# Moving one batch's loads to the SyncE queue and placing every block of loads behind the last transposes of the batch before

## The chip, the cores and the metric

The kernel runs on one core of one Trainium2 chip. The metric is the device time of one launch in microseconds; the kernel before took 297.23 us (median of three runs: 297.23, 308.93 and 295.3). Lower is better.

## The reference

Two stages follow each other. The first is a linear attention with cosine position weights, on 8 batches of 8 heads, 576 positions and head size 64. The second is a feed-forward layer with a squared ReLU.

```python
r = np.maximum(x, 0.0)                       # x is q or k
phi = np.concatenate([r * cos, r * sin], -1)  # 64 -> 128 features
kv = np.einsum('bhsf,bhsd->bhfd', k_p, v)
z = np.sum(k_p, axis=2)
num = np.einsum('bhsf,bhfd->bhsd', q_p, kv)
den = np.einsum('bhsf,bhf->bhs', q_p, z)[..., None] + 1e-06
attn = num / den                              # [8, 8, 576, 64]
x = attn.transpose(0, 2, 1, 3).reshape(4608, 512)
out = np.maximum(x @ w_in, 0.0) ** 2 @ w_out  # 512 -> 2048 -> 512
```

q, k and v hold 9.4 MB each, the two weights 4.2 MB each, and the output 9.4 MB, all in float32.

## The kernel before, in words

**Tiling.** One batch at a time goes through everything. Its 576 positions are cut into four blocks of 128 (the main part) and a tail of 64. The main part of q, k or v is one transfer of 1 MB; the tail is two transfers of 64 KB. There is one buffer each for k, v, q and their tails (`POOLS`, "k": 1 and so on), so the loads of a batch can start only once the features of the preceding batch have been read out of these buffers.

**Attention of a batch (`declare_att`).** VectorE and ScalarE make the cosine and sine features of k and q and cast v to bf16 (`declare_feature`, `declare_v`). TensorE forms the product of k features and v (`declare_kz`), and ScalarE copies it out (`kvz`). The q features must be turned round so that features lie on partitions: for batch 2 and later a DMA transpose on the SyncE queue does this (`declare_qT`, L531: two of 512 KB and one small one, `qpT` and `qpTt`). TensorE then forms numerators and denominators (`declare_num`), VectorE divides and writes `x`, and `x` is turned round by DMA transposes again (`declare_xT`, L620: two of 256 KB and a small one, `xT` and `xTt`). Batches 0 and 1 use TensorE transposes instead.

**Feed-forward of a batch.** Stage one (times `T1[b]`) multiplies `xT` by the first weight, stage two (times `T2[b]`) multiplies the squared ReLU `gT` by the second. Batches 0 to 2 use plain products in stage one (`declare_plain`), later ones a scheme with seven products instead of eight (`declare_seven1`, fed by the sums `xs` of `declare_x_sums`); stage two has rows (`declare_rows`) for the first and pairs with seven products (`declare_pair`) for the rest. In time the attention of batch b+2 lies beside stage two of batch b and stage one of batch b+1.

**Order.** Nothing here is ordered by hand. Each operation is declared with its engine, an estimated duration, the buffers it reads and writes, and for some a position in time (`pos`). `Planner.plan` then goes through them as a list scheduler and emits them in the order of its own clock; after that every engine runs its list in order, and waits on semaphores where data is not there. If an estimate is wrong, an engine stands at the head of its list while later work that is ready waits behind. For DMA the planner has one line of transfers (`pipe`) for all queues: each transfer begins when the one before is done.

**Queues.** Loads come from two places. Loads of batches 0 to 3 go out from GpSimd's queue (q0 in the profile, software_dynamic), except the k of batch 0; the loads of batches 4 to 7 go out from SyncE's queue (q1, hardware_dynamic), which also carries all DMA transposes. The output stores go out from GpSimd's queue, except at the very end. The loads carry a `pos`: batch 3 is declared at `T2[0] + 10`, the k and v of batch b+2 at `T2[b-1] + 10` and its q at `T1[b] + 8.7`; before that time the planner doesn't place them, and from then on it places them as soon as their buffer is free.

Of the kernel before, what the change touches and what calls it, by code (L numbers as in the profile page):

```python
# [34 lines left out]
class Planner:  # L35
# [19 lines left out]
        self.turns.setdefault(pool, []).append(b)  # L55
        return b

    def add(self, engs, fn, r=(), w=(), pos=None, lat=None, size=None):
        if isinstance(engs, tuple):
            engs = {engs[0]: engs[1]}  # L60
        if size:
            lat = 1.5 + size
        op = Op(engs, fn, pos, lat, size)
        for k in r:
            if k in self.writer:
                op.deps.add(self.writer[k])
            self.readers.setdefault(k, []).append(op)
        for k in w:
            if k in self.writer:
                op.deps.add(self.writer[k])  # L70
            op.deps.update(x for x in self.readers.get(k, ()) if x is not op)
            self.writer[k], self.readers[k] = op, []
        for k in list(r) + list(w):
            b = k[0] if isinstance(k, tuple) else k
            if isinstance(b, Buf) and b not in op.bufs:
                op.bufs.append(b)
                b.users += 1
        self.ops.append(op)
        return op

# [26 lines left out]
    def plan(self, t0):  # L107
        ops = self.ops
        for n, op in enumerate(ops):
            op.n = n  # L110
            for d in op.deps:
                d.succ.append(op)
        pe = sorted((o for o in ops if "PE" in o.engs), key=lambda o: (o.pos, o.n))
        t = t0["PE"]
        for o in pe:
            o.late = o.slot = t
            t += o.engs["PE"]
        for o in reversed(ops):
            d = max(o.engs.values()) + (o.lat or 0.16)
            for s in o.succ:  # L120
                o.late = min(o.late, s.late - d)
            if "PE" not in o.engs:
                ends = [
                    s.slot + s.engs["PE"]
                    for s in o.deps
                    if "PE" in s.engs and any(b in s.bufs for b in o.bufs if b.pool in "FB")
                ]
                if ends:
                    o.late = min(o.late, max(ends) + 1.0)
        clock = dict(t0)  # L130
        waiting = {o: len(o.deps) for o in ops}
        pipe = 0.0
        ready = {e: [] for e in clock}
        order = []

        def arm(o):
            for e in o.engs:
                ready[e].append(o)

        for o in ops:  # L140
            if not o.deps:
                arm(o)
        left = len(ops)
        head = 0
        while left:
            best = None
            while head < len(pe) and pe[head].start is not None:
                head += 1
            for e in clock:
                cand = []  # L150
                for o in ready[e]:
                    if e == "PE" and o.slot > pe[head].slot + self.window:
                        continue
                    s = max(clock[e], o.pos if e not in ("PE",) and o.pos else 0.0)
                    for d in o.deps:
                        s = max(s, d.end if d.eng == e and e in ("PE", "ACT", "DVE") else d.done)
                    s = self.room(o, s)[0]
                    if s is not None:
                        cand.append((s, o))
                if not cand:  # L160
                    continue
                s0 = min(c[0] for c in cand)
                s, o = min(
                    (c for c in cand if c[0] <= s0 + 1e-9),
                    key=lambda c: (c[1].slot if e == "PE" else c[1].late, c[1].n),
                )
                if best is None or s < best[0]:
                    best = (s, e, o)
            if best is None:
                stuck = [o for o in pe if o.start is None][:6]  # L170
                raise RuntimeError(f"stuck: {[(o.fn.__name__, o.pos, o.n) for o in stuck]}")
            s, e, o = best
            for x in o.engs:
                ready[x].remove(o)
            o.eng, o.start, o.end = e, s, s + o.engs[e]
            o.done = o.end + (o.lat if o.lat is not None else 0.17 if e == "PE" else 0.09) + self.HOP
            if o.size:
                pipe = o.done = max(o.end + 1.5, pipe) + o.size
            clock[e] = o.end
            for b, i in self.room(o, s)[1]:  # L180
                b.i = i
                self.free[b.pool] = [f for f in self.free[b.pool] if f[1] != i]
            for b in o.bufs:
                b.users -= 1
                b.last = max(getattr(b, "last", 0.0), o.done)
                if b.users == 0:
                    self.free[b.pool].append((b.last, b.i))
            for x in o.succ:
                waiting[x] -= 1
                if not waiting[x]:  # L190
                    arm(x)
            order.append(o)
            left -= 1
        return order
# [3 lines left out]
def kernel(  # L198
# [17 lines left out]
    J = S // P  # L216
# [186 lines left out]
    add = plan.add  # L403
# [6 lines left out]
    T1, T2, t = {}, {}, 16.8  # L410
# [8 lines left out]
            d[key] = plan.buf(pool)  # L419
        return d[key]  # L420

    def declare_load(b, nm, eng, pos=None):
        src = {"k": k, "v": v, "q": q}[nm]
        queue = nc.sync if eng == "SP" else nc.gpsimd
        for part, fn, cost, size in ((nm, load_main, 0.7, 2.9), (nm + "t", load_tail, 1.4, 0.7)):
            buf = loaded[part, b] = plan.buf(part)

            def load(_, fn=fn, buf=buf):
                fn(src, nm, buf.i, b, queue)

            add((eng, cost), load, w=[buf], pos=pos, size=size)

    def source(nm, b, j):
        return loaded[nm if j < J else nm + "t", b]
# [22 lines left out]
    def xT_of(b, half):  # L457
        return cached(xTb, (b, half), "xT")
# [64 lines left out]
    def declare_qT(b, i):  # L523
        n = 2 if i < J // 2 else 1
        src = qp_of(b, 2 * i)
        dst = qpTb[b, i] = plan.buf("qpT" if n == 2 else "qpTt")

        def qT(_):
            s = at(src)
            s = s.rearrange("p r h f -> p (r h f)" if n == 2 else "p h f -> p (h f)")  # L530
            nc.sync.dma_start_transpose(out=at(dst), in_=s)  # L531

        keys = [(src, (2 * i + r) % 2, c) for r in range(n) for c in "cs"]
        add(("SP", 1.7 if n == 2 else 1.2), qT, r=keys, w=[dst], size=1.8 if n == 2 else 0.5)

    def declare_qT_pe(b, j, pos, engs):
        nh = H if j < J else HH
# [65 lines left out]
    def declare_xT(b, i):  # L603
        src = x_of(b, 2 * i)
        if i < J // 2:
            dst, keys = xT_of(b, i), [(src, 0), (src, 1)]
            wkeys = [(dst, 0), (dst, 1)]
        else:
            dst, keys = xTt_of(b), [(src, 0)]
            wkeys = [(dst, b % 4)]  # L610

        def xT(_):
            if i < J // 2:
                o = at(dst).rearrange("p k (r c) -> p (k r) c", r=2)
                s = at(src).rearrange("p k r c -> p (k r c)")
            else:
                o = at(dst)[:, b % 4].rearrange("p k g c -> p (k g) c")
                o = at(dst)[:, b % 4].rearrange("p k g c -> p k (g c)")
                s = at(src).rearrange("p k c -> p (k c)")
            nc.sync.dma_start_transpose(out=o, in_=s)  # L620

        add(("SP", 1.6 if i < J // 2 else 1.2), xT, r=keys, w=wkeys, size=1.0 if i < J // 2 else 0.5)

    def declare_xT_pe(b, j, pos, engs):
        nk = KB if j < J else 2
# [61 lines left out]
            r=[rt], w=[gkey(hb, half)],  # L687
        )

    gttb = {}  # L690

    def declare_tails(b, hb, pos):

# [444 lines left out]
            declare_plain(1, s % 4 * 4 + 2 * i, s // 4, T1[1] + s * 2 * PROD2 + i * PROD2, s == 0)  # L1138
    declare_att(2, T2[1], [T2[1] + x for x in (1.7, 3.4, 5.1, 7.0, 9.0)], DVE1, DVE1, BOTH)
    for nm in "qkv":  # L1140
        declare_load(3, nm, "POOL", T2[0] + 10)
    declare_rows(1, (0, 1), T2[1], 2)
    declare_w2_sums()
    declare_pair(1, 1, T2[1] + 16 * PROD1)
# [5 lines left out]
    for b in range(2, B):  # L1150
        if b > 2:
            if b in SEVEN:
                declare_x_sums(b)
                for r in range(4):
                    declare_seven1(b, r, T1[b] + r * 7 * PROD1)
            for m, first, n in TAILS[b]:
                for i in range(first, first + n):
                    declare_tails(m, 2 * i, T2[b] - 1.5 + 0.01 * i)
        if b + 2 < B:
            for nm in "kv":  # L1160
                declare_load(b + 2, nm, "SP", T2[b - 1] + 10)
            declare_load(b + 2, "q", "SP", T1[b] + 8.7)
            declare_att(b + 2, T2[b] + 5.5, [T1[b + 1] + 0.3 + 1.75 * j for j in range(NS)])
        for i, pair in enumerate(PAIRS[b]):
            declare_pair(b, pair, T2[b] + i * 7 * PROD2)
# [35 lines left out]
```

## Time and profile before

| what | value |
|---|---|
| three runs | 297.23, 308.93, 295.3 us |
| span of the profiled execution | 311.6 us (that run took 313.36 us) |
| TensorE matmul busy | 276.9 us, 89% of the span |
| VectorE, ScalarE, GpSimd busy | 219.3, 191.3, 46.1 us |
| q1 (SyncE's queue) | 63104 packets, 26.22 MB, 44.5% of the 16 DMA engines' time |
| q0 (GpSimd's queue) | 10544 packets, 26.22 MB, 29.8% |

The busy shares are means over the whole span. TensorE is the busiest engine, and the work is laid out around it, so what counts is where TensorE stands still and why. In the rows with forty slices each digit stands for 7.8 us. The row PEclk gives the clock that TensorE was granted; it falls where TensorE has stood still, and matmuls then take longer. In timelines, the bracket at the end of a line says how long the engine was idle before it and whose work ended that.

### The profile page before, as it was taken

To read this page: it belongs to the slowest core of one execution; us is meant where nothing else is said; L and a number is where in the kernel's file an instruction comes from. 1 tells how busy PE (TensorE), PEld (TensorE's weight loads), DVE (VectorE), ACT (ScalarE), POOL (GpSimd) and SP (SyncE) were. 2 spreads that over 40 slices of the span, in tenths; PEclk is the share of its full clock that TensorE was granted. 3 is DMA by queue.
4 is the path that set the end of the run, shared out by engine and by line. 5 is a ranking of instruction groups with operands and counts; after the bars stand their busy time and mean duration, and the time that the engine had idled before them with its cause. 6 is when DMAs were issued, how large, how long until landed. Compare 5 with 4: busy or idle time off the path is not lost.

```text
span 311.6 us, 7075 instructions
## 1 busy us (share of the span) xinstructions
PE 276.9 (89%) x2827; PEld 226.8 (73%) x2827; DVE 219.3 (70%) x513; ACT 191.3 (61%) x378; POOL 46.1 (15%) x76
## 2 busy tenths in 40 slices
PE   8699999991199948987999989989999999999994
PEld 3379756881048936876878878878888887888883
DVE  2669999950275508937998599869984789449851
ACT  3576917960386647618997995699532673386421
POOL 8625272620000000000000000010002000000012
PEclk9999999998579979999999999999999999999999
DMA  7999997899949998699979997955803520110014
GB/s 242 294 206 326 290 307 246 274 140 174 99 76 215 259 166 199 127 210 373 199 163 250 233 179 155 358 135 140 141 14 105 120 43 2 67 69 2 1 69 135
DMA packets 73825, 53.02 MB, mean 170 GB/s; under 512 B 50496, under 2 KB 68416, under 8 KB 73792
## 3 DMA queue, kind: packets, MB, share of 16 engines
q1 hardware_dynamic: 63104, 26.22, 44.5%
q0 software_dynamic: 10544, 26.22, 29.8%
q8 instruction: 22, 0.36, 0.5%
q10 hardware_dynamic: 144, 0.13, 0.1%
q14 instruction: 11, 0.09, 0.1%
HBM read 36.70 MB, written 9.44 MB: 148 GB/s over the span
## 4 chain that ended last, share of the span: by engine, by line
PE 47%; DMA 25%; DVE 17%; ACT 4%; issue 3%; SPq 2%; POOL 2%; POOLq 0%; DVEq 0%; ACTq 0%
PE banks L395 45%; DMA v<-in_v_dram 10%; DMA vt<-in_v_dram 7%; DMA q<-in_q_dram 5%; DVE gT L384 4%; DVE gs L392 2%; DVE rs L387 2%; DVE qp L373 2%; DMA xTt<-xt 1%; ACT rt L381 1%; SPq L531 1%; DVE x L592 1%; DVE w1s L392 1%; ACT rs L381 1%; PE banks L544 1%
## 5 line engine op out<-in xcount | busy, mean ns | idle before, releaser
L395 PEld LDWEIGHTS <-w1sb 128*128 128x128 bf16 x784 | 73.5, 99 | 15.2 <-DMA xT<-x 4.3
L395 PE MATMUL banks<-xT,w1sb 128*128 128x256 bf16 (+1 forms) x576 | 70.0, 270 | 4.7 <-DMA xT<-x 4.0
L395 PE MATMUL banks<-w2sb,gT 128*128 128x256 bf16 (+1 forms) x304 | 52.8, 315 | 13.7 <-ACT rt L381 13.2
L395 PEld LDWEIGHTS <-gT 128*128 128x128 bf16 x408 | 38.8, 99 | 27.9 <-issue 17.4
L395 PEld LDWEIGHTS <-gs 128*128 128x128 bf16 x480 | 46.4, 98 | 10.2 <-issue 4.1
L381 ACT ACTIVATE rt<-banks 128x512 bf16<-128x512 f32 x64 | 37.2, 597 | 19.9 <-PE banks L395 13.7
L356 POOL DMA_DIRECT2D out_dram<-ysb x15 | 8.3, 551 | 218.3 <-DVE ysb L392 112.8
L395 PEld LDWEIGHTS <-w1s 128*128 128x128 bf16 x320 | 30.7, 98 | 6.9 <-issue 3.2
L384 DVE TENSOR_TENSOR gT<-rt 128x512 bf16<-128x512 bf16 x48 | 19.5, 419 | 22.4 <-ACT rt L381 22.2
L395 PE MATMUL banks<-w2sb,gs 128*128 128x256 bf16 x240 | 31.0, 273 | 3.6 <-DVE ysb L392 1.9
L395 PE MATMUL banks<-w2s,gs 128*128 128x256 bf16 x240 | 30.2, 273 | 0.2
L384 DVE TENSOR_TENSOR gT<-rs 128x1024 bf16<-128x1024 bf16 (+1 forms) x50 | 28.3, 579 | 2.4 <-ACT rs L381 1.8
L387 DVE CUSTOM_DVE_ANT_0 rs<-banks,sums 128x512 bf16<-128x512 f32 x40 | 27.1, 684 | 3.3 <-ACT sums L793 2.5
L392 DVE TENSOR_TENSOR ysb<-banks,sums 128x256 f32<-128x256 f32 x30 | 12.6, 420 | 20.6 <-ACT sums L907 10.3
L378 ACT CAST vx<-v 128x512 bf16<-128x512 f32 x22 | 13.6, 623 | 18.6 <-DMA v<-in_v_dram 18.6
L381 ACT ACTIVATE rs<-banks 128x512 bf16<-128x512 f32 x40 | 23.2, 608 | 2.8 <-PE banks L395 2.8
L371 ACT ACTIVATE kp<-k,sin_col 128x512 bf16<-128x512 f32 x32 | 22.0, 721 | 3.4 <-DMA k<-in_k_dram 3.4
L395 PE MATMUL banks<-xT,w1s 128*128 128x256 bf16 x160 | 22.3, 272 | 1.9 <-DVE rs L387 1.7
L371 ACT ACTIVATE qp<-q,sin_col 128x512 bf16<-128x512 f32 x32 | 22.9, 729 | 1.9 <-DMA q<-in_q_dram 1.7
L395 PE MATMUL banks<-xs,w1s 128*128 128x256 bf16 x160 | 23.4, 273 | 0.0
L592 DVE TENSOR_TENSOR x<-banks,den 128x512 bf16<-128x512 f32 x30 | 20.7, 691 | 1.0
L392 DVE TENSOR_TENSOR gs<-gT 128x1024 bf16<-128x1024 bf16 x26 | 17.9, 688 | 2.8 <-PE banks L395 2.3
(106 smaller groups left out, 382.1 us busy)
## 6 DMA issues: line engine op xcount, KB each, us to landing
out_dram<-ysb POOLq DMA_DIRECT2D x15, 512.0 KB, 5.5
k<-in_k_dram SPq DMA_DIRECT2D x5, 1024.0 KB, 6.0
v<-in_v_dram POOLq DMA_DIRECT2D x4, 1024.0 KB, 12.7
v<-in_v_dram SPq DMA_DIRECT2D x4, 1024.0 KB, 9.4
q<-in_q_dram SPq DMA_DIRECT2D x4, 1024.0 KB, 8.0
q<-in_q_dram POOLq DMA_DIRECT2D x3, 1024.0 KB, 9.4
k<-in_k_dram POOLq DMA_DIRECT2D x3, 1024.0 KB, 7.7
w1sb<-in_moe_w_in_dram POOLq DMA_DIRECT2D x4, 512.0 KB, 9.2
```

The source lines that it names most:

```text
L356: eng.dma_start(out=dst, in_=y.rearrange("p i c -> p (i c)") if n > 1 else y[:, c0:c1])
L371: nc.scalar.activation(out=dst, in_=src, func=ACTF.Relu, scale=col)
L373: nc.vector.tensor_scalar(out=dst, in0=src, scalar1=0.0, scalar2=col, op0=ALU.max, op1=ALU.mult)
L378: (nc.scalar.copy if eng == "ACT" else nc.vector.tensor_copy)(out=out, in_=in_)
L381: nc.scalar.activation(out=out, in_=in_, func=ACTF.Relu)
L384: nc.vector.tensor_tensor(out=out, in0=in_, in1=in_, op=ALU.mult)
L387: nc.vector._custom_dve(TENSOR_ADD_SAT, out=out, in0=in0, in1=in1, s0=float("inf"), s1=0.0)
L392: nc.vector.tensor_tensor(out=out, in0=in0, in1=in1, op=op)
L395: nc.tensor.matmul(out=out, lhsT=lhsT, rhs=rhs, start=start, stop=stop, skip_group_check=True)
L531: nc.sync.dma_start_transpose(out=at(dst), in_=s)
L544: nc.tensor.transpose(t[:, h, :], qp_at(b, j)[:, h, :], ident[:, :])
L592: nc.vector.tensor_tensor(out=x_at(b, j).rearrange("p (b k) (l d) -> p b k l d", b=n, l=2), in0=n4[:, :, :, 0:D].rearrange("p b (k l) d -> ...
```

## The change

The loads of batch 3 move from GpSimd's queue to SyncE's. And no load from batch 3 on has a position in time any more: the k and v loads of batch b+2 are declared to come after the last q transpose of batch b+1 (`turned["q", b + 1, J // 2]`, the small `qpTt`), and its q load after the last x transpose of batch b+1 (`turned["x", b + 1, J // 2]`, the small `xTt`). For batch 3, all of k, v and q come after the last q transpose of batch 2, which is the first batch with DMA transposes. The aim is that loads and transposes lie in one queue, one block behind the other, instead of running beside each other.

`after` is an order for the planner alone: it reads `d.end`, the time at which the preceding transpose has been issued, not the time at which it has landed, and no buffer is shared by it. So it adds no wait on the chip beyond the place in SyncE's list.

```diff
-    def add(self, engs, fn, r=(), w=(), pos=None, lat=None, size=None):
+    def add(self, engs, fn, r=(), w=(), pos=None, lat=None, size=None, after=()):
...
+        op.after = set(after) - op.deps
+        op.deps |= op.after
         self.ops.append(op)
...
                     for d in o.deps:
-                        s = max(s, d.end if d.eng == e and e in ("PE", "ACT", "DVE") else d.done)
+                        ordered = d in o.after or d.eng == e and e in ("PE", "ACT", "DVE")
+                        s = max(s, d.end if ordered else d.done)
...
-            add((eng, cost), load, w=[buf], pos=pos, size=size)
+            add((eng, cost), load, w=[buf], pos=pos, size=size, after=after)
...
-        add(("SP", 1.7 if n == 2 else 1.2), qT, r=keys, w=[dst], size=1.8 if n == 2 else 0.5)
+        turned["q", b, i] = add(("SP", 1.7 if n == 2 else 1.2), qT, r=keys, w=[dst], size=1.8 if n == 2 else 0.5)
...
-        add(("SP", 1.6 if i < J // 2 else 1.2), xT, r=keys, w=wkeys, size=1.0 if i < J // 2 else 0.5)
+        turned["x", b, i] = add(("SP", 1.6 if i < J // 2 else 1.2), xT, r=keys, w=wkeys, size=1.0 if i < J // 2 else 0.5)
...
     for nm in "qkv":
-        declare_load(3, nm, "POOL", T2[0] + 10)
+        declare_load(3, nm, "SP", after=[turned["q", 2, J // 2]])
...
             for nm in "kv":
-                declare_load(b + 2, nm, "SP", T2[b - 1] + 10)
-            declare_load(b + 2, "q", "SP", T1[b] + 8.7)
+                declare_load(b + 2, nm, "SP", after=[turned["q", b + 1, J // 2]])
+            declare_load(b + 2, "q", "SP", after=[turned["x", b + 1, J // 2]])
```

What this does to SyncE's list of instructions can be read from the built kernels. Before, from batch 2 on: the two `qpT` and the `qpTt` of batch 2, `vt` of batch 4, `xT` of 2, `qpT` of 3, k and v of 4, `xT` of 2, `qpT` and `qpTt` of 3, `kt` of 4, q and `qt` of 4, `xTt` of 2, `xT` of 3, and so on, with loads and transposes mixed. After: the three q transposes of 2, then k, v, q, `kt`, `vt`, `qt` of 3 in one block, `xT` of 2, `qpT` of 3, `xT` of 2, `qpT` and `qpTt` of 3, then k, v, `kt`, `vt` of 4, then `xTt` of 2 and the x transposes of 3, then q and `qt` of 4, then the q transposes of 4, and so on. (The one exception to whole blocks: an `xT` of batch 4 lies between q and `qt` of batch 5.) GpSimd's list loses the nine transfers of batch 3 and keeps the earlier loads, the weights and the stores. The lists of the other engines keep their work and change a little in order.

More of the change, by code (lines that the diff above doesn't have):

```diff
@@ L420, in cached, with declare_load @@
         return d[key]
-    def declare_load(b, nm, eng, pos=None):
+    def declare_load(b, nm, eng, pos=None, after=()):
         src = {"k": k, "v": v, "q": q}[nm]
@@ L688, in declare_plain @@
         )
-    gttb = {}
+    gttb, turned = {}, {}
     def declare_tails(b, hb, pos):
```

## The prediction

> **What bounds the kernel now.** I read the forty slices of the page first, then the chain that ended last, then the timelines of TensorE, ScalarE, GpSimd and SyncE at the places where the slices show a hole.
>
> ```profile
> PE   8699999991199948987999989989999999999994
> PEclk9999999998579979999999999999999999999999
> DMA  7999997899949998699979997955803520110014
> PE 47%; DMA 25%; DVE 17%; ACT 4%; issue 3%; SPq 2%; POOL 2%; POOLq 0%; DVEq 0%; ACTq 0%
> ```
>
> TensorE is full nearly everywhere. The one deep hole is in slices 10 and 11 (70 to 86 us), a shallow one in slice 14 (109 to 117 us), and after each its clock is down. DMA is full up to slice 25, and a quarter of the chain is DMA. So the kernel is bound by TensorE, with DMA nearly as full in its first two thirds; what can be won is TensorE's waits. The timelines of TensorE and ScalarE show who ends them:
>
> ```profile
> 84.54 2.72 PE L395 MATMUL banks<-w2sb,gT 128*128 128x512 bf16 x6 [13.22 <-ACT rt L381]
> 90.59 1.89 PE L395 MATMUL banks<-w2sb,gT 128*128 128x512 bf16 x8
> 113.45 1.72 PE L395 MATMUL banks<-xT,w1sb 128*128 128x256 bf16 x8 [3.98 <-DMA xT<-x]
> ...
> 82.58 0.62 ACT L378 CAST vx<-v 128x512 bf16<-128x512 f32 x1 [14.01 <-DMA v<-in_v_dram]
> ```
>
> TensorE waits 13.22 us for a ReLU on ScalarE that had its input long before; ScalarE stood at the cast of batch 3's v, one place ahead in its list, 14.01 us for the load. The load and what shares the DMA engines with it (GpSimd's timeline, then SyncE's, then an undisturbed stretch of SyncE's):
>
> ```profile
> 58.54 1.15 POOL L323 DMA_DIRECT2D v<-in_v_dram  x1 [2.66 <-ACT rt L381]
> 62.14 0.91 POOL L323 DMA_DIRECT2D q<-in_q_dram  x1
> ...
> 57.15 26.52 SPq L531 DMA_TRANSPOSE qpT<-qp  x2
> 83.76 2.59 SPq L531 DMA_TRANSPOSE qpTt<-qpt  x1
> 97.56 1.12 SPq L323 DMA_DIRECT2D v<-in_v_dram  x1
> 98.77 6.08 SPq L620 DMA_TRANSPOSE xT<-x  x1
> 104.96 8.02 SPq L531 DMA_TRANSPOSE qpT<-qp  x1
> ...
> 216.41 6.53 SPq L531 DMA_TRANSPOSE qpT<-qp  x2
> ```
>
> v is issued at 58.5 and read at 82.6: 24 us for 1 MB. In the same stretch SyncE hands out two q transposes and needs 26.52 us for it; later the same pair takes 6.53 us with its waits. Loads on q0 and transposes on q1 run beside each other there, and both crawl. The second wait (3.98 us) is `xT` of batch 2, issued at 98.77 behind k and v of batch 4 on one queue. What DMA moves in each case, by windows (the last three columns are TensorE's clock, the DMA share and GB/s):
>
> ```profile
> 62.00:70.00 8.00, 8.00 (x81) 7.09 (x79) 4.77 (x12) 5.13 (x9) 2.29 (x4) 1.00 1.28 149
> 78.00:84.50 6.50, 0.00 (x0) 0.00 (x0) 0.77 (x2) 1.92 (x5) 0.00 (x0) 0.50 1.24 103
> 99.20:106.00 6.80, 6.80 (x80) 6.16 (x78) 2.76 (x7) 3.56 (x7) 0.56 (x1) 1.00 0.99 302
> 217.60:220.20 2.60, 2.60 (x27) 2.33 (x25) 2.57 (x7) 2.60 (x6) 0.00 (x0) 1.00 1.08 201
> ```
>
> Mixed: 149 and 103 GB/s with engines over full. Loads alone (k and v of batch 4): 302. One q transpose alone: 201, so 0.52 MB in 2.6 us.
>
> **What the Trainium skill says.** "DMA: Bandwidth & Descriptors", section "Queues, rings and completion order": each DMA engine goes round the queue rows that have work, a packet at a time. The trace agrees in kind: a transpose consists of packets under 512 B (50496 of 73825 packets on the page are), and beside another queue it waits a turn for each; that the total rate halves as well goes beyond fair turns. The same page, "Issuing engines are not separate DMA queues": transfers from all issuing engines share 16 DMA engines, so a second queue adds no rate. Agrees: 149 GB/s with two, 302 with one. "TensorE: Matmul & The Clock Gate", "Part 1: The HAM clock gate": after an idle window of about 3.4 us the array's clock is halved until it has been busy as long. Agrees: 8 matmuls of 128x512 take 1.89 us at 90.59, and 6 take 2.72 at 84.54.
>
> **The change part by part.**
>
> *Removed: the first wait, and the half clock behind it.* The wait is 13.22 us. At half clock, 6 wide matmuls took 2.72 instead of 6/8 x 1.89 = 1.42, and the next 8 took 3.00 instead of 1.89; with eight small ones (0.64 for 0.41) that is 2.6. Together 15.9 us.
> Now the new order of this stretch, by hand. The q features of batch 2 are ready at 61.7 as before. Two q transposes at 2.6 us and the small one at about 0.65 (a quarter), the first behind the output stores until about 62, end near 68. k, v, q at 1.05 MB / 302 GB/s = 3.5 us each reach 71.5, 75 and 78.5, the six tails at about 0.2 us 80. The cast of v is now placed behind ScalarE's ReLUs and the copy of `kvz`, and behind three k features, which it would reach at about 72 + 3 x 0.6 = 74. Remaining wait: 0 to 2 us, and no ReLU that TensorE needs by then lies behind it, only the copies of the rows after about 77.
>
> *How much of it the median run pays.* The profiled run took 313.36, the median 297.23: 16.1 less, and the first group is 15.9. I read this as: the median run doesn't pay the first wait, because there the two queues get through in time. So this part may be worth nothing against 297.23.
>
> *Removed: the second wait.* `xT` of batch 2, second half, no longer stands behind 2 MB of batch 4 (2.1 MB / 302 GB/s = 6.9 us), since these now follow the q transposes of batch 3. Wait 3.98; half clock 113.45 to 117: 8 matmuls 1.72 for 1.04, 16 in 2.71 for 1.91, small ones 0.64 for 0.41, 1.7; and two waits of 0.82 and 0.70 for the division, which VectorE does only after 7.07 us at `kt` of batch 4, in the same jam. Together 7.2. It is no part of the 15.9, so the median run may still pay it: 297.2 - 7.2 = 290.0. Bounds: 0 (it was a consequence of the first wait) to 7.2.
>
> *Moved: nine issues from GpSimd to SyncE.* About 3 x 0.6 and 6 x 0.6 = 5.4 us of SyncE's time between 64 and 70, while SyncE waits for nothing else. GpSimd's stores gain; it idles most of the time. Zero.
>
> *Moved: k and v of the next batch behind `qpTt`, in front of the x transposes.* Loads of 2 x 3.5 + 0.8 = 7.8 us lie in front of `xT`. Batch 4's x transposes in the trace are done near 153, the sums `xs` that read them run at 160.4, so 7.7 us are free. Nothing up to there.
>
> *Moved: q of the next batch behind `xTt`.* The q load of batch 4 was issued at 115.8, before the x transposes of batch 3 (121.08 and 131.33); now it goes out behind them. Behind it is a row of work: load 4.7 us from issue to landing, features 0.6 each on ScalarE, q transposes 3.8 and 2.6, then the numerators, which TensorE takes in order and for which all its products wait. This is the added wait that the trace of before doesn't show. Lower bound: 0, the planner's list puts numerators behind other products. Upper bound: 2 to 2.5 us for each of batches 4 to 7, one transfer of 0.5 MB beside a store, so 10. I take 0.5 in all, since before, too, loads were late there (waits of 1.92, 0.66 and 1.54 us at 141, 180 and 204 with loads at the head of ScalarE's or VectorE's list), and shorter, unmixed transfers win as much as later issues lose.
>
> Sum: 297.2 - 7.2 + 0.5 = 290.5.
>
> **The rivals.**
>
> *No change, 296.5.* The second wait follows from the first, since everything behind a 16 us hole meets in one place; a run without the first has neither. Then only new small waits count: -1.5 for the better DMA rate, +0.8 for later q loads. For it: the near equality of 16.1 and 15.9 leaves no room for savings elsewhere, and one run was at 295.3. Against: k and v stood ahead of that `xT` in SyncE's list in any run.
>
> *Better, 285.* Besides the 7.2, the three later waits (1.92 + 0.66 + 1.54 = 4.1) go, and 1 us of small ones: 297.2 - 12.3. For it: all three have a late load or its transpose in the list ahead. Against: output stores still run beside the transposes on the other queue.
>
> *Slower, 305.* The row x transpose, q load, features, q transpose, numerators, x transpose becomes a circle that hardly fits into a batch: 4.7 + 1.5 + 6.4 + 7.8 of k and v + about 3 of numerators + 4 of x transposes = 27 us, against 30 to 36 us in the trace from one batch's first x transpose to the next one's (145.5, 175.7, 208.1, 244.0). It fits with 3 us left at the tightest; a store in the middle, or features delayed by a full ScalarE, and TensorE waits 2 to 2.5 us in each of four batches, with nothing won: 297 + 8. Against: in the trace the transposes are a whole stage ahead of their readers.
>
> **How the numbers follow.** 290.5: 0.42; no change 296.5: 0.25; 285: 0.20; 305: 0.13. The limits of 2% are 291.3 and 303.2. The case at 290.5 has some 3 us of spread, so 0.24 of its 0.42 lie below 291.3; with 0.20 that is 0.44 faster. Same: 0.18 + 0.25 = 0.43. Slower 0.13. The range must take in 285 with its spread and reach past 296.5: 283 to 300; what is left out is the slower case and a little below.
>
> **What would show each step.** No ScalarE wait on v and no hole of TensorE between 70 and 86; two q transposes of batch 2 handed out in under 8 us; k, v and q of batch 3 landing one behind the other by 80. The second `xT` of batch 2 landing before its products, no half clock after 30 us. For the added wait: TensorE waiting for `qpT` or for `kvz` in front of numerators of batch 4 or later, or not. The prediction is wrong if holes of 2 us and more recur once a batch (slower case), or if the runs of before turn out to pay less than 7 us in these two places.

## The result, and the profile after

The changed kernel takes 307.7 us (307.19 to 307.95, four runs), the kernel before 299.25 on the same chip (295.3 to 308.93): 1.038 times, with a 95% interval of 1.032 to 1.045. It is slower. All ratios here compare undisturbed runs of a kernel with undisturbed runs of the kernel before on the same chip; the runs of before are spread from 295 to 316 us, so its medians move from call to call and ratios are the better measure.

The page of the changed kernel, its slices and the chain that ended last:

```profile
PE   8699999999995899968896999959899999999995
PEclk9999999999999799999998999999999999999999
DMA  7999998789799337997399559894663610110015
PE 50%; DVE 20%; DMA 18%; ACT 4%; issue 3%; SPq 2%; POOL 1%; DVEq 0%; POOLq 0%; ACTq 0%
PE banks L398 48%; DMA k<-in_k_dram 9%; DMA q<-in_q_dram 6%; DVE gT L387 5%; DVE rs L390 3%; DMA kt<-in_k_dram 3%; DVE gs L395 2%; DVE qp L376 2%; ACT rt L384 1%; DVE x L595 1%; SPq L534 1%; DVE w1s L395 1%; PE banks L547 1%; ACT kp L374 1%; DVE kp L376 1%
```

The deep hole at 70 to 86 us is gone. In its place are shallower ones about once a batch (around 95, 134, 164 and 202 us), and DMA, which was full nearly everywhere up to 195 us, has gaps there. In the chain v and `vt` have given way to k.

The stretch that was mixed before, in SyncE's timeline:

```profile
57.21 7.37 SPq L534 DMA_TRANSPOSE qpT<-qp  x2
65.94 0.57 SPq L326 DMA_DIRECT2D k<-in_k_dram  x1
66.57 0.56 SPq L326 DMA_DIRECT2D v<-in_v_dram  x1
```

and by windows (last three columns: TensorE's clock, DMA share, GB/s):

```profile
62.00:70.00 8.00, 8.00 (x81) 7.11 (x79) 5.02 (x12) 5.87 (x11) 0.00 (x0) 1.00 0.94 179
70.00:78.00 8.00, 7.29 (x82) 4.12 (x81) 6.18 (x15) 6.75 (x13) 0.00 (x0) 1.00 1.07 348
```

The two q transposes are handed out in 7.37 us instead of 26.52, waits between them included, and the loads of batch 3 move at 348 GB/s between 70 and 78 us, where 172 were moved before. This half of the change does what it is for. What it lost shows in the waits of ScalarE and VectorE on loads (engine, operation and line, what it waited for: us in total, times, longest):

```profile
ACT kp L374 <- DMA k<-in_k_dram: 19.0, 6, 5.5
DVE kp L376 <- DMA k<-in_k_dram: 18.4, 5, 6.2
ACT vx L381 <- DMA v<-in_v_dram: 1.8, 1, 1.8
```

Before, these were 4.4 (ScalarE for k), 7.9 (VectorE for k) and 18.6 (ScalarE for v). Of VectorE's sum some 5 us lie in the prologue in every kernel. The first of the new waits, in SyncE's timeline:

```profile
80.62 2.95 SPq L534 DMA_TRANSPOSE qpT<-qp  x1
83.66 3.10 SPq L623 DMA_TRANSPOSE xT<-x  x1
86.86 3.01 SPq L534 DMA_TRANSPOSE qpT<-qp  x1
89.98 1.89 SPq L534 DMA_TRANSPOSE qpTt<-qpt  x1
91.92 0.58 SPq L326 DMA_DIRECT2D k<-in_k_dram  x1
```

in ScalarE's:

```profile
91.83 0.59 ACT L381 CAST kvz<-banks 128x520 bf16<-128x520 f32 x1 [0.61 <-PE banks L398]
97.97 0.72 ACT L374 ACTIVATE kp<-k,cos_col 128x512 bf16<-128x512 f32 x1 [5.55 <-DMA k<-in_k_dram]
98.59 0.58 ACT L384 ACTIVATE rt<-banks 128x512 bf16<-128x512 f32 x1
```

and in TensorE's:

```profile
100.81 3.32 PE L398 MATMUL banks<-xT,w1sb 128*128 128x256 bf16 x16 [5.17 <-ACT rt L384]
```

Read from the bottom: TensorE waits 5.17 us for a ReLU. The ReLU stands behind a k feature on ScalarE, which waits 5.55 us for k of batch 4. That k is issued at 91.92, behind four transposes which took SyncE 2.95 + 3.10 + 3.01 + 1.89 = 10.95 us to hand out, where the planner had put down 1.7 + 1.6 + 1.7 + 1.2 = 6.2. After the wait TensorE runs at half clock (0.50 of full between 100.3 and 103.7 us), and 16 matmuls take 3.32 us where they take 1.91 at 107.07.

### The profile page after: what moved, and what is told of

It reads as the page before. It is cut to its first block, busy times and chain, and to the rows that moved or that the text cites. A ratio compares the mean times of both kernels' runs of the same rounds, so it can differ in the third digit from the quotient of the medians.

```text
span 305.8 us, 7067 instructions
## 1 busy us (share of the span) xinstructions
PE 276.3 (90%) x2827; PEld 226.9 (74%) x2827; DVE 219.9 (72%) x513; ACT 192.1 (63%) x378; POOL 39.3 (13%) x67
## 4 chain that ended last, share of the span: by engine, by line
PE 50%; DVE 20%; DMA 18%; ACT 4%; issue 3%; SPq 2%; POOL 1%; DVEq 0%; POOLq 0%; ACTq 0%
PE banks L398 48%; DMA k<-in_k_dram 9%; DMA q<-in_q_dram 6%; DVE gT L387 5%; DVE rs L390 3%; DMA kt<-in_k_dram 3%; DVE gs L395 2%; DVE qp L376 2%; ACT rt L384 1%; DVE x L595 1%; SPq L534 1%; DVE w1s L395 1%; PE banks L547 1%; ACT kp L374 1%; DVE kp L376 1%
## 5 line engine op out<-in xcount | busy, mean ns | idle before, releaser
L398 PE MATMUL banks<-w2sb,gT 128*128 128x256 bf16 (+1 forms) x304 | 50.5, 306 | 1.1 <-ACT rt L384 0.6
L398 PE MATMUL banks<-xT,w1s 128*128 128x256 bf16 x160 | 23.2, 275 | 10.8 <-ACT sums L793 8.8
L376 DVE TENSOR_SCALAR kp<-k,cos_col 128x512 bf16<-128x512 f32 x25 | 11.4, 498 | 18.4 <-DMA k<-in_k_dram 18.4
L398 PE MATMUL banks<-xs,w1s 128*128 128x256 bf16 x160 | 24.1, 276 | 0.1
```

What stands on the lines that cost most here:

```text
L376: nc.vector.tensor_scalar(out=dst, in0=src, scalar1=0.0, scalar2=col, op0=ALU.max, op1=ALU.mult)
L398: nc.tensor.matmul(out=out, lhsT=lhsT, rhs=rhs, start=start, stop=stop, skip_group_check=True)
```

## The experiments

My theory after this profile, A: the rule puts k and v of batches 4 to 7 behind the last q transpose; the planner believes they land early and puts their readers into ScalarE's and VectorE's lists right at that time; they land later, and both engines stand with ReLUs behind that TensorE needs. Rivals: B, one queue has too much to carry; C, q behind the x transposes is the cost, by way of the numerators.

**The kernel before once more, for another profile.**

> The kernel before, unchanged, for a profile of its own on the same chip. All theories: 295 to 302 us, as in its earlier runs. Theory A (the first wait of 13 us is an accident of two queues side by side and does not belong to the usual run): no wait of TensorE over 6 us between 70 and 86 us in a profile that is near 297. Theory B (the usual run pays it too): the wait is there, 10 us or more.

Measured 305.96 us (301.98 to 308.03). The profiled run took 307.81, and the first wait was in it, by TensorE's timeline:

```profile
80.60 2.72 PE L395 MATMUL banks<-w2sb,gT 128*128 128x512 bf16 x6 [10.70 <-ACT rt L381]
```

The time is above the expected 295 to 302. Since the profiled run wasn't near 297, it doesn't separate the two theories. It shows that the wait comes again, in another size: 10.7 us instead of 13.2. It also shows how far a ratio can be trusted: against 24 more runs of the same kernel on the same chip (295.48 to 311.46) these four have a ratio of 1.021 (1.009 to 1.033), with nothing changed. So differences under 2% are close to the noise below, above all for a kernel whose loads of batch 3 still run on the other queue.

**Each half alone.** First, only batch 3 moves; the loads of batches 4 to 7 keep their old positions:

```diff
-                declare_load(b + 2, nm, "SP", after=[turned["q", b + 1, J // 2]])
-            declare_load(b + 2, "q", "SP", after=[turned["x", b + 1, J // 2]])
+                declare_load(b + 2, nm, "SP", T2[b - 1] + 10)
+            declare_load(b + 2, "q", "SP", T1[b] + 8.7)
```

> Only the first half of the change: batch 3 goes to SyncE's queue behind the q transposes of batch 2; the loads of batches 4 to 7 keep their positions in time. Theory A (the time is lost because k and v of batches 4 to 7 are placed behind the last q transpose, land late, and ScalarE and VectorE stand at the head of their lists for k): 290 to 298 us, and the waits on k go from 19 and 18 us (ScalarE, VectorE) to under 10 each. Rival B (SyncE's queue has too much to carry once batch 3 is on it): 304 us or more. Rival C (late q loads behind the x transposes): as A, it can't be told apart here.

297.29 us, ratio 0.998 (0.994 to 1.002). Then only the rule, batch 3 as before:

```diff
-        declare_load(3, nm, "SP", after=[turned["q", 2, J // 2]])
+        declare_load(3, nm, "POOL", T2[0] + 10)
```

> Only the second half: batch 3 stays on GpSimd's queue with its position in time, the loads of batches 4 to 7 follow the preceding batch's last transposes. Theory A: 304 to 312 us, waits on k once a batch as in the changed kernel. Rival B (batch 3 on SyncE's queue is the cost): 294 to 299 us.

309.51 us, ratio 1.031 (1.020 to 1.042). The waits on k, first in the kernel with only batch 3 moved:

```profile
ACT kp L374 <- DMA k<-in_k_dram: 3.7, 4, 1.6
DVE kp L376 <- DMA k<-in_k_dram: 7.4, 3, 4.9
```

and then in the one with only the rule:

```profile
ACT kp L374 <- DMA k<-in_k_dram: 19.7, 6, 6.0
DVE kp L376 <- DMA k<-in_k_dram: 16.8, 4, 6.7
```

The loss is in the rule, whole, and B falls. The second kernel also bears on what the repeated profile of before left open: it has the same loads of batch 3 on the same queue beside the same transposes of batch 2, and in its profile TensorE's wait there was this:

```profile
71.20 1.46 PE L398 MATMUL banks<-w2sb,gT 128*128 128x512 bf16 x6 [1.61 <-ACT rt L384]
```

So the first wait can be 1.6 or 13 us with the same placement of these transfers; it differs from execution to execution. In this one the loads went first: between 62 and 70 us the packets of GpSimd's queue took 96.3% of the DMA engines' time and those of SyncE's 6.9%, at 277 GB/s in all. In the profile of before the shares were 65.0 and 62.0%, at 149 GB/s. What decides this stays open.

**Which loads.** The rule undone for k and v alone (q stays behind the x transposes):

> The changed kernel, but k and v of batches 4 to 7 go by their old position in time; q stays behind the x transposes. Theory A (k placed behind the last q transpose and read at once is the cost): 291 to 299 us, waits on k well under half of the 19 and 18 us of the changed kernel. Rival C (q behind the x transposes is the cost): 304 to 309 us.

290.46 us, ratio 0.974 (0.967 to 0.982), a little below the range of theory A. Waits on k: 2.9 and 8.8 us. The mirror image, undone for q alone:

> The mirror image: q of batches 4 to 7 by its old position in time, k and v behind the last q transpose. Theory A: 303 to 309 us, waits on k as in the changed kernel. Rival C: 291 to 299 us.

303.52 us, ratio 1.021 (1.012 to 1.030). Waits on k: 14.8 and 15.7 us. With batch 3 moved in all four, the two halves of the rule make a square of ratios:

| | q by position | q behind the x transposes |
|---|---|---|
| k and v by position | 0.998 | 0.974 |
| k and v behind the last q transpose | 1.021 | 1.038 |

k and v behind the last q transpose cost in both columns, and C falls as the main cause. But the two halves don't add up. k and v cost 6.4% of the time of before where q stands behind the x transposes (1.038 less 0.974), and 2.3% where q goes by position. q behind the x transposes costs 1.7% where k and v are late already, and gains 2.4% where they are not. That gain isn't explained: ScalarE's waits on loads are shorter there (on v 5.0 us instead of 8.0, on q 3.4 instead of 4.7), but no run separates the causes.

**Late data or a list that trusts too early.** The order on SyncE's queue stays but for two `xT`, and the planner believes the loads of batches 4 to 7 to land 4 us later:

```diff
                 pipe = o.done = max(o.end + 1.5, pipe) + o.size
+                o.done += o.slack
...
-            add((eng, cost), load, w=[buf], pos=pos, size=size, after=after)
+            op = add((eng, cost), load, w=[buf], pos=pos, size=size, after=after)
+            op.slack = 4.0 if b > 3 else 0.0
```

> The changed kernel, but the planner believes the loads of batches 4 to 7 to land 4 us later than it did; the order of loads and transposes on SyncE's queue stays (but for one xT of batch 3 and one of batch 4), and features and casts move back in the lists of ScalarE and VectorE. Theory A1 (what costs is not that k lands late but that its features stand at the head of the lists before it lands): 290 to 299 us, waits on k under 8 us on each engine. Rival A2 (data are needed by then, so the wait moves to TensorE in front of the products of k and v or the numerators): 303 to 309 us. Rival B (DMA is the bound): no change, 306 to 309 us.

291.89 us, ratio 0.982 (0.968 to 0.995). Waits on k:

```profile
ACT kp L376 <- DMA k<-in_k_dram: 5.3, 4, 2.0
DVE kp L378 <- DMA k<-in_k_dram: 6.7, 2, 5.1
```

and ScalarE's timeline at the place of the first wait:

```profile
90.85 0.60 ACT L386 ACTIVATE rt<-banks 128x512 bf16<-128x512 f32 x1 [0.38 <-PE banks L400]
...
93.47 0.60 ACT L386 ACTIVATE rt<-banks 128x512 bf16<-128x512 f32 x1 [0.28 <-PE banks L400]
96.08 0.72 ACT L376 ACTIVATE kp<-k,cos_col 128x512 bf16<-128x512 f32 x1 [2.02 <-DMA k<-in_k_dram]
```

Four ReLUs now go ahead of the k feature, and the wait is 2.02 us instead of 5.55. TensorE nowhere waits for a k feature in that profile, so k came early enough for its products; the lists had asked for it too early. With 2 us instead of 4:

> The changed kernel, all loads of batches 4 to 7 believed 2 us later instead of 4. Theory A: the lists still run into k by 1 to 4 us a batch, so between the two, 294 to 301 us. Rival A4 (any change of the lists is enough, the old one was an unlucky order): 290 to 293 us.

300.26 us, ratio 1.009 (1.000 to 1.017); waits on k 12.4 and 13.2 us. With 0, 2 and 4 us of belief the ratio goes 1.038, 1.009, 0.982: 5.6% or about 16 us for 4 us in each of four batches. The even step speaks against a lucky order. The kernels with 2 and 4 us have exactly the same order on SyncE's queue, so the 2.7% between them come from the lists of the other engines.

**Is it k?** The belief for k and its tail alone:

```diff
-            op.slack = 4.0 if b > 3 else 0.0
+            op.slack = 4.0 if b > 3 and nm == "k" else 0.0
```

> The changed kernel, and the planner believes only k and its tail of batches 4 to 7 to land 4 us later; v and q as it did. Theory A (k is the load that the lists run into, since it is the first of its block): near the 291.9 of the run with all loads believed later, 290 to 297 us. Rival E (v and q cost as much): 299 us or more.

307.47 us (304.25 to 309.66), ratio 1.026 (1.013 to 1.038). My expectation was wrong. The waits, from a profile of a 309.0 us run:

```profile
ACT vx L383 <- DMA v<-in_v_dram: 13.0, 4, 5.3
ACT kp L376 <- DMA k<-in_k_dram: 3.1, 3, 1.3
```

The k features step back as asked, the casts of v step forward to the head of ScalarE's list, and stand there instead. So it isn't k alone that costs; the whole block is late, and this profile fits that whatever of it is first in a list pays.

**Why the block is late.** The planner's four costs for SyncE's transposes set to their means in the changed kernel's trace:

```diff
-add(("SP", 1.7 if n == 2 else 1.2), qT, ...
+add(("SP", 2.4 if n == 2 else 1.4), qT, ...
-add(("SP", 1.6 if i < J // 2 else 1.2), xT, ...
+add(("SP", 2.0 if i < J // 2 else 1.4), xT, ...
```

> The changed kernel with four numbers of the planner set to the means that SyncE's issues took in its trace: qpT 2.4 instead of 1.7, qpTt 1.4 instead of 1.2, xT 2.0 instead of 1.6, xTt 1.4 instead of 1.2. Theory A3 (k comes late because SyncE needs longer for the transposes ahead of it than the planner thinks): most of the loss is regained, 292 to 300 us. Rival A4 (the lateness is in the transfer itself, behind stores and in the fixed part, not in the issue): 303 to 308 us.

295.44 us, ratio 0.992 (0.989 to 0.996); waits on k 4.6 and 7.1 us. These four numbers alone regain 4.6%, of the 5.6 that the 4 us of belief regain. They also change the order of a few transfers, and they move the readers of the transposes in the lists as well as those of the loads. So this supports that the issues are what the planner's clock is short by, and doesn't give an exact split.

**How far behind.** k and v behind the first q transpose of the preceding batch instead of the last (`turned["q", b + 1, 0]`):

> The changed kernel, but k and v of batches 4 to 7 come behind the first q transpose of the preceding batch instead of the last. Theory A (what counts is how early k goes out against the place of its features in the lists, and the planner moves the features with it): the transposes that k has to wait for become one or two fewer in some batches only, since k also needs its buffer; some of the loss is regained, 296 to 305 us. Rival D (each block as a whole behind transposes is what costs, the place in it doesn't matter): 306 to 308 us.

302.55 us, ratio 1.018 (1.014 to 1.022): some is regained, as A says. ScalarE still waits 7.5 us for k and 7.1 for v, and TensorE 2.8 for an `xT`.

**Better than both.** Batch 3 on SyncE's queue, all other loads by their old positions, and the belief of 4 us:

> Batch 3 on SyncE's queue, the loads of batches 4 to 7 by position in time (as in the run with only the first half, 297.3), and the planner believes them to land 4 us later. It asks whether taking turns is worth anything once the lists allow for late landings. If taking turns is worth something: 295 to 298 us, clearly over the 291.9 of the run with turns and the same belief. If the belief is all: 290 to 293.5 us.

287.67 us, ratio 0.965 (0.958 to 0.972), the best of all and below both ranges. So the belief gains 3.3% where no load of batches 4 to 7 follows the rule, too, and the 5.6% that it regains in the changed kernel aren't all loss by the rule. The fair comparison is with and without the rule: without the belief the rule costs 4.0% (1.038 less 0.998), with it 1.7% (0.982 less 0.965), and the last is near the noise.

With q behind the x transposes and the belief:

> k and v of batches 4 to 7 by position in time, q behind the x transposes (290.5 without the belief), and all of them believed 4 us later. Is it better than the 287.7 of the run with all loads by position and the belief? If the remaining waits on loads are all that is left: 285 to 288.5 us. If a q behind the x transposes costs something once it is planned still later: 289 to 293 us.

289.56 us, ratio 0.974 (0.970 to 0.978). TensorE waits 3.2 us for `qpT` here, which it doesn't in the best one; so once the lists allow for late loads, a late q does show in front of the numerators, with about 1%, which is within the noise. For k and v the belief takes away nearly everything: behind the last q transpose they cost 6.4% without it, and with it 0.8% (0.982 less 0.974), not clear of noise.

## Why the prediction was wrong, point by point

- **First wait removed: right.** No hole between 70 and 86 us; k, v and q of batch 3 follow one another, and all of them have landed by about 80. Their nine issues took SyncE 9.3 us, from 65.94 to 75.23, where 5.4 were put down.
- **The usual run pays little of it: supported, not shown.** Moving batch 3 alone leaves the ratio at 0.998, and a kernel with the same mixture had 1.6 us there. No run of before near 297 us has a profile. The two that have one took 307.81 and 313.36 us and pay 10.7 and 13.2. Over all runs the medians were 300.34 for before (24 runs) and 297.29 with batch 3 moved (20 runs), so longer runs of before may be those that pay; that isn't shown. The prediction also read 149 GB/s against 302 as two queues against one; with transfers waiting on both queues the other execution moved 277, so a second queue alone doesn't make the jam.
- **Second wait removed, 7.2 us: the wait went, for another reason, and the gain didn't come.** No TensorE wait on `xT` is left in the changed kernel. None is left with only batch 3 moved either, where k and v of batch 4 still go out ahead of the second `xT` of batch 2, the order that the prediction blamed (SyncE's timeline of that run):

```profile
76.21 0.38 SPq L326 DMA_DIRECT2D k<-in_k_dram  x1
79.06 0.55 SPq L326 DMA_DIRECT2D v<-in_v_dram  x1
88.10 1.27 SPq L623 DMA_TRANSPOSE xT<-x  x1
```

That kernel has neither wait, its longest new wait of TensorE there is 2.73 us, and its ratio is 0.998. Either the usual run of before doesn't pay the 7.2, as the rival of no change had argued, or new waits took it back; net, the term measured about 0 instead of 7.2, so this step failed as well. That the kernel with k and v by position takes 290.46, next to the predicted 290.5, is luck: the rule for k and v, which was to bring the 7.2, isn't in it, and its gain comes with q behind the x transposes, which was put at a cost.

- **"Moved: k and v of the next batch behind `qpTt` ... Nothing up to there": this is the step that failed and made the kernel slower.** I asked who reads the transposes that now stand behind the loads, and found 7.7 us of slack. I didn't ask who reads k and v themselves, which now stand behind the transposes. Their readers lie in in-order lists at the time the planner believes in, and the planner's clock for SyncE is short by 4.8 us in front of the first such block (10.95 against 6.2). TensorE's waits that lead back to k or its tail `kt` in the changed profile are 5.17, 2.21, 0.89, 2.94, 2.51 and 1.11, 14.8 us, and two stretches at half clock behind them add about 1.4 us each. Term set: 0; measured by undoing it in the changed kernel: 6.4% or some 17 to 19 us, and 2.3% where q goes by position.
- **q behind the x transposes, 0.5 us: not one number.** It costs 1.7% while k and v are late, gains 2.4% (about 7 us) with k and v by position, and costs about 1%, within the noise, when the belief is added. The prediction weighed later issues against unmixed transfers and set them about equal; that the sign depends on the other loads it didn't see, and why is open.
- **The slower rival: near in size, wrong in cause.** It had 305 us from a circle through the numerators, with TensorE waiting for `qpT`. TensorE waited 0.77 us for a `qpTt`, once.

The Trainium skill says in "DMA: Bandwidth & Descriptors", "Issuing engines are not separate DMA queues", that the issuing sequencer's time is "usually small relative to the DMA itself". For DMA transposes this case disagrees: in the changed kernel SyncE needed 2.4 us on average to hand out a `qpT` that takes 2.6 us to move alone.

## What to carry to other kernels

Where a planner or a hand-written list fixes the order on in-order engines, a load that moves back in its queue moves the readers' place in the lists only as far as the plan believes. Ask of each moved transfer who reads it, how long the issues ahead of it take on the trace, and what stands behind the reader. A margin in the believed landing time is cheap when the data isn't needed yet: 4 us of it gained some 16 us in the changed kernel, and about 10 (0.998 to 0.965) where the loads had kept their places.

## What the runs showed of the hardware that I had not expected

- SyncE's time to hand out a DMA transpose varied with what stood ahead of it in the queue: in the changed kernel 1.23 us for an `xT` alone, 3.10 behind a `qpT` on its way, 4.69 behind a block of loads. No run isolates this, and a small `xTt` took 1.22 right behind such a block.
- Loads on one queue beside transposes on the other fell to 103 to 172 GB/s in one execution, and passed in another with 1.6 us of wait, the loads served first at 277 GB/s. With the loads of batch 3 on SyncE's queue, 20 runs of one kernel lay within 7.5 us and 20 of another within 5.0, where 24 runs of the kernel before spread over 16.0 and 23 over 19.8.
- Half clock didn't follow from the length of one wait. TensorE ran at half clock behind waits of 5.17 and 2.94 us in the changed kernel, and behind one of 1.82 us with k and v by position (16 small matmuls took 1.06 us there, 0.65 elsewhere), but at full clock behind one of 2.51 us in the changed kernel. So the idle time of about 3.4 us that the prediction took over isn't a limit that can be read off single waits here.
